# Running the first unit's half parts one weight piece at a time, with the recurrence between their steps

## The chip, the cores and the metric

The kernel runs on one core of one Trainium2 chip. The metric is the device time of one execution in microseconds (us), as the median of several. Before the change it was 684.3 us (4 runs, 682.91 to 685.18).

All arithmetic is fp32. The engines are TensorE (matrix products, PE in the profile, its weight loads PEld), VectorE (DVE), ScalarE (ACT), GpSimd (POOL), and the queue of transfers (SPq).

## The reference

A decaying recurrence (retention) is followed by a two-layer perceptron with leaky ReLU:

```python
gamma = 1.0 - 2.0 ** (-5.0 - np.arange(H))
for t in range(S):                                  # B=4, H=8, S=768, D=64
    state = gamma * state + einsum('bhd,bhe->bhde', k[:, :, t], v[:, :, t])
    y[:, :, t] = einsum('bhd,bhde->bhe', q[:, :, t], state) / sqrt(D)
x = y.transpose(0, 2, 1, 3).reshape(3072, 512)
h = x @ w_in                                        # (512, 2048)
out = np.maximum(0.01 * h, h) @ w_out               # (2048, 512)
```

The weights arrive as 64-bit floats, which the kernel turns into 32-bit ones itself.

## The kernel before

The sequence is cut into 6 chunks of 128 positions. For chunk c and batch b, TensorE computes **scores** (`ap`), VectorE masks them (`am`), and TensorE adds up three products in one PSUM tile (`yp`): **reads** of the old state (not in chunk 0), **values**, and the new **state**. VectorE then **takes** x and the state out of that tile. GpSimd scales v by decay rates beforehand.

```python
def stage_a(c, b):                       # scores, then the mask
    ps = two_banks(f"ap_{c}_{b}")
    for a in range(HP):
        for j in range(2):
            nc.tensor.matmul(ps[:, j, a, :], lhsT=x[ts(j, 64), 1, a, :], rhs=x[ts(j, 64), 0, a, :])
    nc.vector.tensor_tensor(out=am, in0=ps, in1=mask, op=ALU.mult)     # (views cut)

def stage_y(c, bs, xb):                  # reads, values, state for each b, then the taking
    ...
```

The perceptron works in units of 512 hidden columns. The products of a unit normally go by a scheme of seven block products that needs **sums** of weight blocks and **differences** of x blocks (VectorE work: `add_sums`, `differences`). At the very start those are not ready, so the first unit of chunks 0 and 1 goes directly, as four **half parts** (chunk 0 or 1, `th` = batches 0-1 or 2-3). Weights come in pieces of 512 KB; ScalarE (`next_powers`) and VectorE (`next_mantissas`) convert one piece each.

```python
def direct(c, u, x, g, th):
    for kh in range(2):
        for r in range(2):
            for i in range(2):
                for k in range(2):       # pieces 2*kh and 2*kh+1 alternate
                    nc.tensor.matmul(banks[r][:, i, :], lhsT=block(2*u, r + 2*kh)[:, k, ts(i, 128)],
                                     rhs=x[:, 2*kh + th, k, :], ...)
            if kh == 1: nc.scalar.activation(g[:, 2*r + th], banks[r], AF.Prelu, alpha=0.01)
            yield
```

The main program strings these together by hand, and the trace shows each engine's work in that order (TensorE's: scores at 4.63 us, products at 8.30, scores at 11.06, products at 14.23, half part at 16.64):

```python
for _ in range(3): next_powers()
scored(0, 0)(); read(0, 0)(); scored(0, 1)()
next_mantissas(); next_powers(); read(0, 1)(); next_mantissas()
run(direct(0, 0, xs[0][0], parts[0][1], 0),
    {1: [next_mantissas, next_mantissas, scored(0, 2)], 3: [scored(0, 3)]})
...
read(0, 2)(); read(0, 3)()
run(direct(0, 0, xs[0][0], parts[0][1], 1), {1: [scored(1, 0)], 3: [scored(1, 1)]})
...
read(1, 0, 1)(); next_mantissas(); next_mantissas()
run(direct(1, 0, xs[1][0], parts[1][1], 0), {1: [scored(1, 2)], 3: [scored(1, 3)]})
...
differences(*parts[0][1:]); read(1, 2, 3)(); next_mantissas()
run(direct(1, 0, xs[1][0], parts[1][1], 1), {0: [next_mantissas]})
```

## Time and profile before

| what | value |
|---|---|
| time, median | 684.3 us |
| span of the profiled execution | 682.1 us |
| TensorE busy | 661.7 us (97%) |
| TensorE idle after its first matmul, up to 100 us | 12.1 us |
| VectorE busy | 369.2 us (54%) |
| start of the second half part | 33.87 us |
| start of the first output stage (A_o) | 73.19 us |

The prediction shows the rows for TensorE's waits and for the slow array clock (0.91 and 0.67). Two more rows of TensorE's timeline matter later (start, length, engine, source line, operation, tiles, shapes, number, and in brackets the idle time before):

```profile
99.73 1.97 PE L315 MATMUL B_h<-t,w 128*128 128x256 f32 x8 [0.30 <-DVE w L283]
...
122.46 1.99 PE L315 MATMUL A_o<-g,w 128*128 128x256 f32 x8
```

Groups of this form start every 1.73 us when nothing waits. The first of these two starts 2.18 after the group ahead of it, 0.45 late, and the next one starts 1.81 after it: 0.53 lost for a bracket of 0.30. The second starts 0.20 late without any bracket, and the next one 1.83 after it. So the wait there cost more than its bracket shows. The weight loads stood still ahead of both groups (PEld idle for 0.67 and 0.44 us); that this is the reason was not tested.

### The profile page before, as it was taken

What the parts mean: (1) busy time and instruction counts of PE and PEld (TensorE: products, weight loads), DVE (VectorE), ACT (ScalarE), POOL (GpSimd) and SP (SyncE); (2) the same over time, 40 slices, a digit from 0 to 9 for tenths busy, and PEclk for the clock granted to TensorE, in tenths of its full rate; (3) what the DMA queues carried; (4) which work ended last, traced back from release to release, by engine and by line L of the source; (5) the groups of instructions that cost most, each with busy time, mean ns of one, the idle gap of its engine ahead of it and who ended that gap; (6) DMA issues with size and microseconds to landing.
All of it is one profiled execution on the core that took longest, in us unless ns stands there. A gap on an engine that the chain in (4) does not pass through costs nothing.

```text
span 682.1 us, 9555 instructions
## 1 busy us (share of the span) xinstructions
PE 661.7 (97%) x4112; PEld 577.8 (85%) x4112; DVE 369.2 (54%) x563; ACT 162.2 (24%) x271; POOL 27.2 (4%) x29
## 2 busy tenths in 40 slices
PE   5888999999999999999999999999999999999997
PEld 4677888888888888888888888888888888888886
DVE  3637898988888765703653533553451354341342
ACT  4122635545542001311210221220221130221210
POOL 1300000000001010100100100100000000000000
PEclk9899999999999999999999999999999999999999
DMA  8901222223412453100301300301300000100001
GB/s 344 380 2 63 93 93 93 89 66 124 153 34 92 124 184 123 67 0 13 111 1 63 124 1 0 125 0 62 124 1 0 1 1 16 46 1 0 1 1 62
DMA packets 15161, 49.11 MB, mean 72 GB/s; under 512 B 1680, under 2 KB 1680, under 8 KB 15120
## 3 DMA queue, kind: packets, MB, share of 16 engines
q1 hardware_dynamic: 15120, 48.51, 20.2%
q8 instruction: 32, 0.52, 0.3%
q14 instruction: 9, 0.07, 0.0%
HBM read 42.21 MB, written 6.29 MB: 71 GB/s over the span
## 4 chain that ended last, share of the span: by engine, by line
PE 95%; DVE 3%; DMA 1%; issue 0%; POOL 0%; SPq 0%; DVEq 0%; POOLq 0%
PE A_o L315 12%; PE B_o L315 12%; PE C_o L315 12%; PE B_h L315 11%; PE C_h L315 11%; PE A_h L315 11%; PE D_o L315 6%; PE D_h L315 6%; PE d L333 4%; PE ap L147 4%; PE yp L169 3%; PE yp L164 1%; PE yp L176 1%; DMA dec<-decay_dram 1%; DVE x L182 1%; DVE w L276 0%
## 5 line engine op out<-in xcount | busy, mean ns | idle before, releaser
L315 PE MATMUL A_h<-x,w 128*128 128x256 f32 x352 | 83.2, 379 | 0.0
L315 PEld LDWEIGHTS A_h<-x,w 128*128 128x128 f32 x352 | 66.9, 190 | 9.1
L315 PE MATMUL A_o<-g,w 128*128 128x256 f32 x288 | 68.1, 379 | 0.0
L315 PEld LDWEIGHTS A_o<-g,w 128*128 128x128 f32 x288 | 54.6, 190 | 7.9 <-ACT g L361 0.4
L346 ACT ACTIVATE g<-g 128x512 f32<-128x512 f32 x66 | 40.0, 629 | 75.9 <-DVE g L280 75.9
L280 DVE TENSOR_TENSOR m<-m,B_h 128x512 f32<-128x512 f32 x22 | 15.1, 685 | 56.9 <-PE B_h L315 56.9
L280 DVE TENSOR_TENSOR m<-m,B_o 128x512 f32<-128x512 f32 x16 | 10.9, 684 | 63.9 <-PE B_o L315 63.9
L182 DVE TENSOR_TENSOR x<-yp,dec 128x512 f32<-128x512 f32 x24 | 16.5, 688 | 53.1 <-PE yp L176 40.8
L351 ACT COPY m<-A_h 128x512 f32<-128x512 f32 x22 | 12.8, 583 | 135.6 <-PE A_h L315 97.8
L150 DVE TENSOR_TENSOR am<-ap,mask 128x1024 f32<-128x1024 f32 x24 | 28.6, 1220 | 27.4 <-PE ap L147 27.4
L315 PE MATMUL C_h<-t,w 128*128 128x256 f32 x176 | 42.2, 383 | 0.0
L315 PE MATMUL B_h<-x,w 128*128 128x256 f32 x176 | 42.2, 383 | 0.0
L315 PE MATMUL B_h<-t,w 128*128 128x256 f32 x176 | 41.7, 379 | 0.3 <-DVE w L283 0.3
L315 PE MATMUL D_h<-t,w 128*128 128x256 f32 x176 | 41.6, 379 | 0.0
L315 PE MATMUL C_h<-x,w 128*128 128x256 f32 x176 | 41.6, 379 | 0.0
L133 POOL TENSOR_TENSOR kv<-kv,dec 128x512 f32<-128x512 f32 x19 | 21.0, 1103 | 450.3 <-DMA kv<-in_kv_dram 273.3
L333 PE MATMUL d<-x,w 128*128 128x256 f32 x128 | 31.3, 400 | 7.4 <-DVE x L182 5.2
L315 PEld LDWEIGHTS B_h<-t,w 128*128 128x128 f32 x176 | 33.4, 190 | 5.2 <-issue 0.7
L315 PEld LDWEIGHTS C_h<-x,w 128*128 128x128 f32 x176 | 33.4, 190 | 4.5
L315 PEld LDWEIGHTS D_h<-t,w 128*128 128x128 f32 x176 | 33.4, 190 | 4.5
L315 PEld LDWEIGHTS C_h<-t,w 128*128 128x128 f32 x176 | 32.9, 190 | 5.0
L315 PEld LDWEIGHTS B_h<-x,w 128*128 128x128 f32 x176 | 32.9, 190 | 4.9 <-issue 0.3
(103 smaller groups left out, 1057.1 us busy)
## 6 DMA issues: line engine op xcount, KB each, us to landing
raw<-in_weights_dram SPq DMA_DIRECT2D x31, 512.0 KB, 3.4
qk<-in_qk_dram SPq DMA_DIRECT2D x19, 512.0 KB, 3.8
kv<-in_kv_dram SPq DMA_DIRECT2D x19, 512.0 KB, 4.8
out_dram<-o SPq DMA_DIRECT2D x24, 256.0 KB, 2.1
in<-in_qk_dram SPq DMA_DIRECT2D x3, 512.0 KB, 11.6
in<-in_kv_dram SPq DMA_DIRECT2D x3, 512.0 KB, 11.6
o_in<-in_qk_dram SPq DMA_DIRECT2D x2, 512.0 KB, 10.2
o_in<-in_kv_dram SPq DMA_DIRECT2D x2, 512.0 KB, 10.9
```

What stands on the lines that cost most here:

```text
L133: nc.gpsimd.tensor_tensor(out=v, in0=v, in1=gk.unsqueeze(2).to_broadcast([128, H, D]), op=ALU.mult)
L147: nc.tensor.matmul(ps[:, j, a, :], lhsT=x[ts(j, 64), 1, a, :], rhs=x[ts(j, 64), 0, a, :])
L150: nc.vector.tensor_tensor(out=am.rearrange("p j a t -> p (j a) t"), in0=ps.rearrange("p j a t -> p (j a) t"), in1=mask.unsqueeze(1).to_bro ...
L164: nc.tensor.matmul(ps[ts(i, 64), j, m, :], lhsT=st[b][ts(j, 64), a, :], rhs=x[ts(j, 64), 0, a, :], start=(m == 0), stop=False, skip_group_ ...
L169: nc.tensor.matmul(ps[ts(i, 64), j, m, :], lhsT=y[:, 1, 2 * a + j, :], rhs=am[:, j, a, :], start=(c == 0 and m == 0), stop=True, skip_grou ...
L176: nc.tensor.matmul(sp[ts(j, 64), a, :], lhsT=y[:, 0, 2 * a + j, :], rhs=y[:, 1, 2 * a + j, :], start=False, stop=True, skip_group_check=True)
L182: nc.vector.tensor_tensor(out=blocks, in0=ps[:, :, 0 : HP // 2, :], in1=gq, op=ALU.mult)
L280: nc.vector.tensor_tensor(out=out, in0=a, in1=b, op=ALU.add)
L315: nc.tensor.matmul(ps[:, i, :], lhsT=block(w, sa)[:, k, ts(i, 128)], rhs=rhs[:, k, :], start=(first and i == 0 and n == 0 and k == 0), sto ...
L333: nc.tensor.matmul(banks[r][:, i, :], lhsT=block(2 * u, r + 2 * kh)[:, k, ts(i, 128)], rhs=x[:, 2 * kh + th, k, :], start=(kh == 0 and i = ...
L346: nc.scalar.activation(g[:, i], g[:, i], AF.Prelu, alpha=0.01)
L351: nc.scalar.copy(out=got["m1"], in_=ps)
```

## The change

The intent is to let TensorE work while VectorE masks, takes and converts. It has four parts.

1. A half part goes in four steps, each with the four matmuls of one weight piece, which leave eight records in the trace (x8 in the row at 20.86 us below).
2. The pieces of the recurrence (`score`, `masked`, `reads`, `values`, `state`, `taken`) become functions of their own, and the program puts steps of a half part between them.
3. The sums of weights and the differences of x of this unit move from the output stages to places between the half parts.
4. The decay table goes in two transfers, 6 KB of rates ahead of the first kv and 256 KB later, and the order of later transfers shifts.

```diff
-        for kh in range(2):
-            for r in range(2):
-                for i in range(2):
-                    for k in range(2):
+        for step in range(4):
+            kh, k = divmod(step, 2)
+            for r in range(2):
+                for i in range(2):
...
+    load(0, 0, between=lambda: nc.sync.dma_start(out=dec[:, rates:], in_=decay[:, rates:]))
+    load(0, 1, between=lambda: nc.sync.dma_start(out=dec[:, :rates], in_=decay[:, :rates]))
...
     scored(0, 0)()
-    read(0, 0)()
+    products(0, [0])
     scored(0, 1)()
-    next_mantissas()
-    next_powers()
-    read(0, 1)()
+    next_powers()
+    taken(0, 0, x)
+    products(0, [1])
+    taken(0, 1, x)
+    next_powers()
     next_mantissas()
...
+    steps = direct(0, 0, x, parts[0][1], 1)
+    next(steps)
+    scored(1, 0)()
+    next(steps)
+    scored(1, 1)()
...
+    next(steps)
+    products(1, [0, 1])
+    next_mantissas()
+    run(steps, {})
...
+    taken(1, 0, x1)
+    taken(1, 1, x1)
+    last_difference(x)
```

More of the change, by code (lines that the diff above doesn't have):

```diff
@@ L115, with load @@
     AHEAD = 2
-    def load(c, b, place=None):
+    def load(c, b, place=None, between=lambda: None):
         if place is None:
@@ L126, in load @@
             y = flat[:, half : 2 * half].rearrange("p (s h d) -> p s h d", s=2, h=H)
+        heads[c, b] = x, y
         nc.sync.dma_start(out=x, in_=qk[c, b])
+        between()
         nc.sync.dma_start(out=y, in_=kv[c, b])
-        heads[c, b] = x, y
     def decay_v(c, b):
@@ L134, in decay_v, with score @@
                                 op=ALU.mult)
-    scores = {}
+    scores, sums_at = {}, {}
     def two_banks(name):
         return psum.tile([128, 2, HP, C], FP32, tag="att", bufs=2, name=name)
-    def stage_a(c, b):
+    def score(c, b):
         x = heads[c, b][0]
-        ps = two_banks(f"ap_{c}_{b}")
+        ps = scores[c, b] = two_banks(f"ap_{c}_{b}")
         for a in range(HP):
@@ L148, in stage_a, with masked @@
                                  rhs=x[ts(j, 64), 0, a, :])
-        am = scores[c, b] = work.tile([128, 2, HP, C], FP32, tag="am", bufs=2, name=f"am_{c}_{b}")
+    def masked(c, b):
+        am = work.tile([128, 2, HP, C], FP32, tag="am", bufs=2, name=f"am_{c}_{b}")
         nc.vector.tensor_tensor(
-            out=am.rearrange("p j a t -> p (j a) t"), in0=ps.rearrange("p j a t -> p (j a) t"),
+            out=am.rearrange("p j a t -> p (j a) t"),
+            in0=scores[c, b].rearrange("p j a t -> p (j a) t"),
@@ L152, in stage_a @@
             in1=mask.unsqueeze(1).to_broadcast([128, H, C]), op=ALU.mult)
-    def stage_y(c, bs, xb):
-        got = [(b, *heads.pop((c, b)), scores.pop((c, b)), two_banks(f"yp_{c}_{b}")) for b in bs]
-        more = c < NC - 1
-        pairs = [(j, m, i, 2 * m + i) for m in range(HP // 2) for j in range(2) for i in range(2)]
-        sums = {}
-        for b, x, _, _, ps in got:
-            for j, m, i, a in pairs if c > 0 else ():
-                nc.tensor.matmul(ps[ts(i, 64), j, m, :], lhsT=st[b][ts(j, 64), a, :],
-                                 rhs=x[ts(j, 64), 0, a, :], start=(m == 0), stop=False,
-                                 skip_group_check=True)
-        for _, _, y, am, ps in got:
-            for j, m, i, a in pairs:
-                nc.tensor.matmul(ps[ts(i, 64), j, m, :], lhsT=y[:, 1, 2 * a + j, :],
-                                 rhs=am[:, j, a, :], start=(c == 0 and m == 0), stop=True,
-                                 skip_group_check=True)
-        for b, _, y, _, ps in got:
-            sp = sums[b] = ps[:, 0, HP // 2 :, :].rearrange("p a (two d) -> p (a two) d", two=2)
-            for a in range(HP) if more else ():
-                for j in range(2):
-                    nc.tensor.matmul(sp[ts(j, 64), a, :], lhsT=y[:, 0, 2 * a + j, :],
-                                     rhs=y[:, 1, 2 * a + j, :], start=False, stop=True,
-                                     skip_group_check=True)
-        for b, _, _, _, ps in got:
-            th, o = divmod(b * C, N)
-            blocks = xb.rearrange("p (kh th) k n -> p kh th k n", th=2)[:, :, th, :, ds(o, C)]
-            nc.vector.tensor_tensor(out=blocks, in0=ps[:, :, 0 : HP // 2, :], in1=gq, op=ALU.mult)
-            sp = sums[b]
-            if more:
-                if c > 0:
-                    nc.vector.tensor_tensor(out=st[b], in0=st[b], in1=sp, op=ALU.add)
-                nc.vector.tensor_tensor(out=st[b], in0=st[b] if c > 0 else sp,
-                                        in1=gc.unsqueeze(2).to_broadcast([128, HP, D]),
-                                        op=ALU.mult)
@@ new lines, in masked, with reads @@
+        scores[c, b] = am
+    pairs = [(j, m, i, 2 * m + i) for m in range(HP // 2) for j in range(2) for i in range(2)]
+    def reads(c, b):
+        x = heads[c, b][0]
+        ps = sums_at[c, b] = two_banks(f"yp_{c}_{b}")
+        for j, m, i, a in pairs if c > 0 else ():
+            nc.tensor.matmul(ps[ts(i, 64), j, m, :], lhsT=st[b][ts(j, 64), a, :],
+                             rhs=x[ts(j, 64), 0, a, :], start=(m == 0), stop=False,
+                             skip_group_check=True)
@@ new lines, in values, with for_state, state @@
+    def values(c, b):
+        y, am, ps = heads[c, b][1], scores.pop((c, b)), sums_at[c, b]
+        for j, m, i, a in pairs:
+            nc.tensor.matmul(ps[ts(i, 64), j, m, :], lhsT=y[:, 1, 2 * a + j, :],
+                             rhs=am[:, j, a, :], start=(c == 0 and m == 0), stop=True,
+                             skip_group_check=True)
+    def for_state(ps):
+        return ps[:, 0, HP // 2 :, :].rearrange("p a (two d) -> p (a two) d", two=2)
+    def state(c, b):
+        y = heads.pop((c, b))[1]
+        sp = for_state(sums_at[c, b])
+        for a in range(HP) if c < NC - 1 else ():
+            for j in range(2):
+                nc.tensor.matmul(sp[ts(j, 64), a, :], lhsT=y[:, 0, 2 * a + j, :],
+                                 rhs=y[:, 1, 2 * a + j, :], start=False, stop=True,
+                                 skip_group_check=True)
@@ new lines, in taken @@
+    def taken(c, b, xb):
+        ps = sums_at.pop((c, b))
+        th, o = divmod(b * C, N)
+        blocks = xb.rearrange("p (kh th) k n -> p kh th k n", th=2)[:, :, th, :, ds(o, C)]
+        nc.vector.tensor_tensor(out=blocks, in0=ps[:, :, 0 : HP // 2, :], in1=gq, op=ALU.mult)
+        sp = for_state(ps)
+        if c < NC - 1:
+            if c > 0:
+                nc.vector.tensor_tensor(out=st[b], in0=st[b], in1=sp, op=ALU.add)
+            nc.vector.tensor_tensor(out=st[b], in0=st[b] if c > 0 else sp,
+                                    in1=gc.unsqueeze(2).to_broadcast([128, HP, D]), op=ALU.mult)
@@ L190, in stage_y, with products @@
+    def products(c, bs):
+        for f in (reads, values, state):
+            for b in bs:
+                f(c, b)
+    def stage_y(c, bs, xb):
+        products(c, bs)
+        for b in bs:
+            taken(c, b, xb)
             n = c * B + b + AHEAD
@@ L283, in minus, with add_sums, last_sum, differences @@
         nc.vector.tensor_tensor(out=out, in0=a, in1=b, op=ALU.subtract)
-    def add_sums(k):
+    def add_sums(k, last=True):
         a11, a21, a12, a22, s1, s2, s4 = (block(k, i) for i in range(7))
         plus(s1, a21, a22)
-        minus(a21, a11, a21)
         minus(s2, s1, a11)
         minus(s4, a12, s2)
-    def differences(x, t):
+        if last:
+            last_sum(k)
+    def last_sum(k):
+        minus(block(k, 1), block(k, 0), block(k, 1))
+    def differences(x, t, last=True):
         minus(t[:, 0], x[:, 1], x[:, 0])
@@ L296, in differences, with last_difference @@
         minus(t[:, 2], x[:, 2], t[:, 1])
+        if last:
+            last_difference(x)
+    def last_difference(x):
         minus(x[:, 1], x[:, 3], x[:, 1])
@@ L328, in direct @@
                  for r in range(2)]
-        for kh in range(2):
+        for step in range(4):
+            kh, k = divmod(step, 2)
             for r in range(2):
                 for i in range(2):
-                    for k in range(2):
-                        nc.tensor.matmul(
-                            banks[r][:, i, :], lhsT=block(2 * u, r + 2 * kh)[:, k, ts(i, 128)],
-                            rhs=x[:, 2 * kh + th, k, :], start=(kh == 0 and i == 0 and k == 0),
-                            stop=(kh == 1 and k == 1), skip_group_check=True)
-                if kh == 1:
+                    nc.tensor.matmul(
+                        banks[r][:, i, :], lhsT=block(2 * u, r + 2 * kh)[:, k, ts(i, 128)],
+                        rhs=x[:, 2 * kh + th, k, :], start=(step == 0 and i == 0),
+                        stop=(step == 3), skip_group_check=True)
+                if step == 3:
                     nc.scalar.activation(g[:, 2 * r + th], banks[r], AF.Prelu, alpha=0.01)
-                yield
+            yield
     def hidden(c, u, x, t, g, gd):
@@ L453, in do @@
             decay_v(c, b)
-            stage_a(c, b)
+            score(c, b)
+            masked(c, b)
         return do
@@ L470, in rounds @@
         return {i: [round_piece] for i in steps}
-    load(0, 0)
-    nc.sync.dma_start(out=dec, in_=decay)
-    load(0, 1)
-    for n in range(3):
-        load_piece(n)
+    rates = HP * C
+    load(0, 0, between=lambda: nc.sync.dma_start(out=dec[:, rates:], in_=decay[:, rates:]))
+    load(0, 1, between=lambda: nc.sync.dma_start(out=dec[:, :rates], in_=decay[:, :rates]))
+    load_piece(0)
+    load_piece(1)
+    load(0, 2, new_o("in2"))
+    load_piece(2)
     load_piece(3, tile_x("words").rearrange("p i k n -> p (i k n)")[:, 0 : 2 * W])
-    load(0, 2, new_o("in2"))
     load(0, 3, new_o("in3"))
@@ L481 @@
     load(1, 1, unit_tile(LATE[1], "in11"))
+    load(1, 2, unit_tile(LATE[0], "in12"))
     nc.vector.memset(mask, 1.0)
@@ L484 @@
                             base=0, pattern=[[1, 128]], channel_multiplier=-1)
-    for _ in range(3):
-        next_powers()
     xs = {0: new_x(0)}
@@ L492 @@
     parts = [new_g(0, 0)]
+    x, t = xs[0]
     scored(0, 0)()
-    read(0, 0)()
+    products(0, [0])
     scored(0, 1)()
+    next_powers()
[3 more added lines that the diff above has]
+    next_powers()
     next_mantissas()
     next_powers()
-    read(0, 1)()
-    next_mantissas()
-    run(direct(0, 0, xs[0][0], parts[0][1], 0),
-        {1: [next_mantissas, next_mantissas, scored(0, 2)], 3: [scored(0, 3)]})
-    load(1, 2, unit_tile(LATE[0], "in12"))
-    load(1, 3)
-    read(0, 2)()
-    read(0, 3)()
-    run(direct(0, 0, xs[0][0], parts[0][1], 1), {1: [scored(1, 0)], 3: [scored(1, 1)]})
-    next_powers()
+    load(1, 3)
+    scored(0, 2)()
+    steps = direct(0, 0, x, parts[0][1], 0)
+    next(steps)
+    reads(0, 2)
+    values(0, 2)
+    next_mantissas()
+    decay_v(0, 3)
+    score(0, 3)
+    state(0, 2)
+    next(steps)
+    next_mantissas()
+    masked(0, 3)
+    next_powers()
+    taken(0, 2, x)
+    next_mantissas()
+    next(steps)
+    reads(0, 3)
+    values(0, 3)
+    state(0, 3)
+    run(steps, {})
+    taken(0, 3, x)
+    add_sums(0, last=False)
+    differences(x, t, last=False)
+    steps = direct(0, 0, x, parts[0][1], 1)
+    next(steps)
+    scored(1, 0)()
+    next(steps)
+    scored(1, 1)()
+    next_powers()
+    next_mantissas()
+    next_powers()
+    next(steps)
+    products(1, [0, 1])
+    next_mantissas()
+    run(steps, {})
     next_powers()
@@ L510 @@
     parts.append(new_g(1, 0))
-    read(1, 0, 1)()
+    x1, t1 = xs[1]
+    taken(1, 0, x1)
+    taken(1, 1, x1)
+    last_difference(x)
+    scored(1, 2)()
+    steps = direct(1, 0, x1, parts[1][1], 0)
+    next(steps)
+    scored(1, 3)()
+    next(steps)
+    differences(*parts[0][1:])
+    next(steps)
+    products(1, [2, 3])
     next_mantissas()
+    next_powers()
+    run(steps, {})
+    taken(1, 2, x1)
+    taken(1, 3, x1)
     next_mantissas()
-    run(direct(1, 0, xs[1][0], parts[1][1], 0), {1: [scored(1, 2)], 3: [scored(1, 3)]})
     next_powers()
+    differences(x1, t1, last=False)
+    run(direct(1, 0, x1, parts[1][1], 1), {1: [next_mantissas]})
     next_powers()
-    differences(*parts[0][1:])
-    read(1, 2, 3)()
-    next_mantissas()
-    run(direct(1, 0, xs[1][0], parts[1][1], 1), {0: [next_mantissas]})
-    next_powers()
-    next_powers()
+    last_sum(0)
     differences(*parts[1][1:])
+    last_difference(x1)
     for u in range(NU):
@@ L535 @@
             at = rounds(1, 4) if u < NU - 1 else {}
-            if u == 0:
-                put(at, s2=[differ(c)])
-                if c == 0:
-                    put(at, s3=[lambda: add_sums(0)])
+            if u == 0 and c == 0:
+                at = rounds(4)
             if u == NU - 1 and NC > 2:
```

## The prediction

> **What bounds the kernel now.** I read the page first, then TensorE's timeline over the first 100 us, then VectorE's over the same stretch, then the view of busy time by stretch.
>
> ```profile
> PE 661.7 (97%) x4112; PEld 577.8 (85%) x4112; DVE 369.2 (54%) x563; ACT 162.2 (24%) x271; POOL 27.2 (4%) x29
> ...
> PE   5888999999999999999999999999999999999997
> ```
>
> TensorE is busy for 661.7 of 682.1 us, so all its idle time is 20.4 us, 3.0% of the span. The row by slices says where: the first four slices (17 us each) hold nearly all of it. The change touches the code up to about 100 us only, and leaves the number of matmuls alone. What it can win is idle time there, and clock.
>
> ```profile
> 14.23 1.09 PE L169 MATMUL yp<-am,kv 128*64 128x128 f32 x16 [1.38 <-issue]
> ...
> 19.48 4.85 PE L333 MATMUL d<-x,w 128*128 128x256 f32 x14 [2.14 <-DVE w L276]
> ...
> 33.87 3.72 PE L333 MATMUL d<-x,w 128*128 128x256 f32 x16 [0.78 <-DVE x L182]
> ...
> 44.76 0.67 PE L164 MATMUL yp<-in,st 64*64 64x128 f32 x16 [0.73 <-DVE am L150]
> ...
> 50.06 3.69 PE L333 MATMUL d<-x,w 128*128 128x256 f32 x16 [1.80 <-DVE x L182]
> ...
> 66.21 7.15 PE L333 MATMUL d<-x,w 128*128 128x256 f32 x32 [1.80 <-DVE x L182]
> ```
>
> The number in brackets is TensorE's idle time before the group, and what ended it. Of all brackets in this view: 4.63 for the first load, then 1.59, 1.38, 0.85, 2.14, 0.78, 0.73, 1.80, 0.73, 1.80 and, at 99.73, 0.30. After the first matmul that is 12.1 us. The two pairs of 0.73 and 1.80 have one form: scores (ap) are followed at once by the recurrence (yp), which waits for the mask on VectorE; and the recurrence is followed at once by a half part (d), which waits for VectorE to bring x out of PSUM. The 2.14 is another: weights not yet converted.
>
> ```profile
> 17.28 0.69 DVE L274 SCALAR_TENSOR_TENSOR w<-raw,w 128x512 f32<-128x512 uint32 x1
> 18.08 1.34 DVE L276 SCALAR_TENSOR_TENSOR w<-w,z 128x512 f32<-128x512 f32 x1
> 19.35 0.41 DVE L272 TENSOR_SCALAR w<-raw 128x512 uint32<-128x512 uint32 x1
> 19.80 0.69 DVE L274 SCALAR_TENSOR_TENSOR w<-raw,w 128x512 f32<-128x512 uint32 x1
> ```
>
> One piece of weights costs VectorE 0.41 + 0.69 + 0.69 and small gaps, some 1.95 us. One here took 1.34.
>
> ```profile
> 16.00:20.00 4.00, 1.22 (x3) 0.80 (x4) 3.83 (x7) 2.58 (x5) 1.44 (x1) 0.91 1.03 406
> 20.00:24.00 4.00, 4.00 (x14) 3.19 (x12) 3.63 (x5) 0.00 (x0) 1.20 (x2) 0.67 1.02 410
> ```
>
> Per stretch: width, then busy time of TensorE, its weight loads, VectorE, ScalarE, GpSimd, then clock. At 16 to 24 us VectorE has 3.83 and 3.63 us of work in 4 us: it is the bound there, not TensorE. The clock falls to 0.91 and 0.67 after the idle 2.14, and the 14 records of d take 4.85 us where 16 take 3.72 later (3.25 for 14): 1.6 us lost.
>
> [...] the first scores take 2.08 us, the later ones 1.16; the dip above costs 3.2 us at half speed. [...] the 1.34 at 18.08 and a 1.41 at 21.66 are the same operations that take 0.69 elsewhere, and GpSimd's value scaling (L133) ran at 17.44 to 18.88 and 21.38 to 22.53. [...] the trace has 680 to 690. So moving sums and differences costs VectorE nothing new, it only changes when.
>
> **The change part by part.** TensorE's pieces, warm, from its timeline: a half part d is 32 records, 7.3 us, now in four steps of 8 records, 1.83 each; scores ap 1.1; one batch's yp of chunk 0 1.55 (values 1.03, state 0.5); the two batches of chunk 1 together 4.16 (43.36 to 48.25 less 0.73). VectorE: mask 1.25, taking x and state of chunk 0 1.1, of chunk 1 1.45, one piece 1.95, one sum or difference 0.69.
>
> *Up to the first half part (now 16.64).* The decay rates that GpSimd needs come in a small transfer of their own before kv, so scaling starts when kv lands instead of at 7.20. But the mask ends at 8.05 anyway, so the first values move from 8.30 to about 8.15: 0.15 won. Then mask(0,1) comes before the taking of (0,0) on VectorE. The second products use the PSUM tile that the taking must free (two buffers, scores and sums in turn). So: scores end 12.75, mask 14.0, taking 15.1, values start at 15.15, not 14.23: 0.9 lost. Products end 16.85; scores of (0,2) fill 16.85 to 18.0.
>
> *The first half part.* VectorE's chain, in program order: taking (0,1) 16.9 to 18.0, piece 0 to 19.95, mask (0,2) to 21.2, piece 1 to 23.2, plus about 0.65 where GpSimd's scaling of a landing kv falls on it, piece 2 to 25.8 (26.4 with a second collision), mask (0,3) to 27.6, taking (0,2) to 28.7, piece 3 to 30.7. TensorE: step 0 at 19.95 (to 21.8), values (0,2), scores (0,3), state (0,2) to 24.5, step 1 to 26.35, step 2 to 28.25, values and state (0,3) from 28.8 to 30.4, step 3 from 30.7 to 32.5. If a cold spell as now falls on it, TensorE is up to 1.6 us later in the middle, of which the waits behind absorb a third or so. I put the start of the second half part at 32.8, against 33.87 now: 1.1 won. TensorE's work is spread between VectorE's, but VectorE's chain from 16.9 to 30.7 is nearly unbroken: it becomes the bound, and so the gain here is small.
>
> *The three other half parts (33.87 to 73.19 now, 39.3).* Work: three times 7.3, four scores 4.4, two double products 8.3: 34.6. The idle in it is 0.73 + 1.80 + 0.73 + 1.80 = 5.06, which accounts for the rest within 0.4. In the new order a step of d (1.83) stands between the scores and the recurrence, against a mask of 1.25: both 0.73 vanish. Between the products and the next half part stand step 3 (1.85) and, after the first pair, scores (1.1): together 2.95 against the 2.15 that VectorE needs until the second x. That 1.80 vanishes too. After the second pair only step 3 stands there, 1.85 against 2.15: 0.3 stays. So 4.8 won by the sum of idle, 4.4 by the difference of span and work; I take 4.4.
>
> *VectorE in that stretch.* Over 28 us after 32.8 it has masks, takings and pieces much as now, plus the six operations of add_sums and differences moved forward (4.1 us). I count 22 to 24 us of work: it fits, with little slack near the end. At the first output stage (A_o, now at 73.19, then about 67.7) VectorE has some 7 us of queue left: part of piece 8, last_sum, four differences, and the last difference of x. The first thing that the stage needs from it, u2, then comes at about 75; TensorE needs that bank again five products later, at 67.7 + 5 x 1.73 = 76.4. It holds by 1.4 us.
>
> *The output stages.* Twelve operations on x and weights (8.2 us) leave them for earlier places, so the wait of 0.30 at 99.73 goes.
>
> Sum: 0.15 - 0.9 is inside the 1.1; 1.1 + 4.4 + 0.3 = 5.8 us of 684.05, so 678.3. After 100 us TensorE has no gap of note (578.4 busy of 582), and nothing there changes.
>
> **Rivals.** (a) *VectorE takes over as the bound from 17 to 76 us.* For it: it is full already at 16 to 24 us, and the new order puts more into 17 to 70. Against: between 33.87 and 48.30 it is busy only 3.19 of 14.43 us, so there is room for all that moves. If it does, the first part wins nothing and u2 comes late: 2 to 3 us won in all, 681.5. (b) *Every gap is closed.* The order of mask and taking at 13 us does no harm, and the clock stays warm because TensorE's work is spread: then the first part wins 3 us or more, 8 in all, 676. Against: piece 0 cannot be ready before VectorE has taken (0,1). (c) *The transfers.* Pieces 4 and later wait for a buffer that piece 0's conversion frees, now some 4 us later, and stand in one queue with the last inputs. Against: before, ScalarE first touches piece 4 at 42.87, VectorE at 50.61, and nothing is in flight from 36 us on; a landing near 30 is early enough for a use near 40. If it went wrong, VectorE would stall at piece 4 and the time would be as now.
>
> **Range and chances.** The certain part is 4 to 5 us (the waits of one form); the first part is worth between -1 and +3. That gives 676.3 to 681.0. Runs of before spread over 682.91 to 685.18, which the range leaves room for. Two per cent is 13.7 us; all the idle after the first matmul is 12.1 and the cold spells add 3 to 4, so faster by 2% would need all of it: 0.01. For slower nothing new is computed: 0.01.
>
> **What would show it.** In the changed trace: A_o starts at 67 to 68.5 instead of 73.19; no waits of TensorE on the mask near 40 to 60 us; one wait of at most 0.5 before the last half part of chunk 1; between 16.9 and 31 us VectorE idle under 2 us, and TensorE's waits there named after weights (L276 now) or the taking; values (0,1) at about 15.1, waiting for the taking. I am wrong if the second half part starts at 34 or later, or at 31 or before; if TensorE waits on u2 or on sums in the output stages; or if a gap appears after 100 us.

Where the text is marked as cut, here and in the expectation of e6, it spoke of the hardware without a trace or run of this case to show it. No term of the sum went with the cuts: it came to 1.1 + 4.4 + 0.3 = 5.8 us. The dip is a granted clock of 0.50 from 19.25 to 22.66 us, 3.2 us of it from the start of the 14 records at 19.48; the trace shows the slow operations of VectorE only as overlapping GpSimd's in time, not why; and 680 to 690 are the ns of one VectorE sum or difference of two 128x512 fp32 tiles (L283).

## The result, and the profile after

| kernel | median us | executions | ratio to before |
|---|---|---|---|
| before | 684.3 | 682.91 to 685.18 (4) | 1 |
| changed | 676.72 | 676.07, 676.70, 676.73, 678.18 | 0.9894 (0.9871 to 0.9917) |

A ratio here is the mean time of one kernel's fast runs over that of the other's of the same rounds, so not quite the ratio of the medians quoted. The measured 676.72 lies inside the predicted 676.3 to 681.0 and 1.6 us below the predicted value. The profiled execution is the slowest of the four (678.18); that turns out to matter.

The page of the changed kernel, the busy time of the engines and the chain that ended last by engine:

```profile
PE 662.4 (98%) x4112; PEld 580.1 (86%) x4112; DVE 371.4 (55%) x563; ACT 162.6 (24%) x271; POOL 27.2 (4%) x29
...
PE 97%; DMA 1%; DVE 0%; issue 0%; POOL 0%; SPq 0%; DVEq 0%; POOLq 0%
```

The same chain in the kernel before, in which VectorE still had 3%:

```profile
PE 95%; DVE 3%; DMA 1%; issue 0%; POOL 0%; SPq 0%; DVEq 0%; POOLq 0%
```

As many TensorE records as before take nearly the same time (662.4 us, 661.7 before), in a span of 676.2 instead of 682.1. TensorE's timeline in the first 100 us:

```profile
8.85 1.97 PE L174 MATMUL yp<-am,kv 128*64 128x128 f32 x16 [2.53 <-POOL kv L134]
...
15.06 1.98 PE L174 MATMUL yp<-am,kv 128*64 128x128 f32 x16 [1.37 <-issue]
...
20.86 3.40 PE L366 MATMUL d<-x,w 128*128 128x256 f32 x8 [1.87 <-DVE w L299]
...
32.29 3.72 PE L366 MATMUL d<-x,w 128*128 128x256 f32 x16
...
59.38 9.02 PE L366 MATMUL d<-x,w 128*128 128x256 f32 x40
68.24 1.89 PE L347 MATMUL A_o<-g,w 128*128 128x256 f32 x8
```

Three brackets remain after the first matmul: 2.53, 1.37 and 1.87. From 20.86 us on there is none up to the output stages: the two pairs of 0.73 and 1.80, the 0.78 and the 0.30 are gone. The row at 32.29 holds step 3 of the first half part and step 0 of the second. The second half part therefore starts at about 34.2, not earlier than before (33.87), while A_o starts at 68.24 instead of 73.19. In this execution everything was won behind 34 us, and nothing in front of it.

The front shows why. Busy time by stretch of four microseconds (TensorE, its weight loads, VectorE, ScalarE, GpSimd, granted clock, share of transfers, GB/s):

```profile
16.00:20.00 4.00, 2.99 (x42) 2.68 (x38) 2.04 (x4) 2.49 (x5) 1.04 (x1) 1.00 1.03 408
20.00:24.00 4.00, 3.14 (x8) 2.21 (x8) 3.76 (x6) 1.26 (x2) 1.04 (x1) 0.66 1.03 410
```

At 20 to 24 us the clock is 0.66, and step 0, eight records, takes 3.40 us; the same eight take 1.99 in the rows at full clock. At 16 to 20 us VectorE has only 2.04 us of work, and then TensorE waits for it:

```profile
13.73 1.23 DVE L153 TENSOR_TENSOR am<-ap,mask 128x1024 f32<-128x1024 f32 x1 [6.07 <-PE ap L148]
14.87 0.68 DVE L195 TENSOR_TENSOR x<-yp,dec 128x512 f32<-128x512 f32 x1
15.47 0.41 DVE L200 TENSOR_TENSOR st<-yp,dec 128x256 f32<-128x256 f32 x1
17.92 0.69 DVE L195 TENSOR_TENSOR x<-yp,dec 128x512 f32<-128x512 f32 x1 [2.04 <-PE yp L186]
18.53 0.41 DVE L200 TENSOR_TENSOR st<-yp,dec 128x256 f32<-128x256 f32 x1
18.86 0.42 DVE L295 TENSOR_SCALAR w<-raw 128x512 uint32<-128x512 uint32 x1
```

VectorE idles for 2.04 us before taking x of (0,1) and begins piece 0 only after it, at 18.86, although ScalarE had finished its part of piece 0 at 14.13. In the kernel before, piece 0 was converted in that gap (14.05 to 15.98).

### The profile page after: what moved, and what is told of

Same layout as the page of the kernel before. It is cut to its first block, busy times and chain, and to the rows that moved or that the text cites. A ratio compares the mean times of both kernels' runs of the same rounds, so it can differ in the third digit from the quotient of the medians.

```text
span 676.2 us, 9567 instructions
## 1 busy us (share of the span) xinstructions
PE 662.4 (98%) x4112; PEld 580.1 (86%) x4112; DVE 371.4 (55%) x563; ACT 162.6 (24%) x271; POOL 27.2 (4%) x29
## 4 chain that ended last, share of the span: by engine, by line
PE 97%; DMA 1%; DVE 0%; issue 0%; POOL 0%; SPq 0%; DVEq 0%; POOLq 0%
PE B_o L347 12%; PE A_o L347 12%; PE C_o L347 12%; PE B_h L347 11%; PE C_h L347 11%; PE A_h L347 11%; PE D_o L347 6%; PE D_h L347 6%; PE d L366 5%; PE yp L174 4%; PE ap L148 3%; PE yp L167 2%; PE yp L186 2%; DMA kv<-in_kv_dram 1%; POOL kv L134 0%
## 5 line engine op out<-in xcount | busy, mean ns | idle before, releaser
L303 DVE TENSOR_TENSOR m<-m,B_h 128x512 f32<-128x512 f32 x22 | 15.1, 686 | 57.1 <-PE B_h L347 57.1
L153 DVE TENSOR_TENSOR am<-ap,mask 128x1024 f32<-128x1024 f32 x24 | 28.6, 1220 | 17.8 <-PE ap L148 17.8
L306 DVE TENSOR_TENSOR gd<-g,gd 128x512 f32<-128x512 f32 x48 | 34.8, 725 | 1.8
```

The costliest lines, as they stand in the source:

```text
L153: nc.vector.tensor_tensor(out=am.rearrange("p j a t -> p (j a) t"), in0=scores[c, b].rearrange("p j a t -> p (j a) t"), in1=mask.unsqueeze ...
L303: nc.vector.tensor_tensor(out=out, in0=a, in1=b, op=ALU.add)
L306: nc.vector.tensor_tensor(out=out, in0=a, in1=b, op=ALU.subtract)
```

## The experiments

The theory after the result: the order of the three later half parts carries 5 us or more of the gain. The front is worth little, because what the interleaving wins there is taken back by the late piece 0, by a later first kv, and by the slow clock. Rivals: the steps by pieces carry the gain; the moved sums and differences carry it; or the clock alone does. Twelve kernels were run, all in five rounds, all correct. The medians of the kernel before were 684.66, 684.57 and 684.75.

| label | what it is | median us | lowest to highest | ratio (95% interval) |
|---|---|---|---|---|
| e1_front_only | new front, old later part | 682.46 | 682.44 to 682.93 | 0.9970 (0.9958 to 0.9983) |
| e6_steps_only | before, with steps by pieces | 682.21 | 680.67 to 683.51 | 0.9961 (0.9947 to 0.9976) |
| e2_front_old | old front with steps, new later part | 675.33 | 674.49 to 676.93 | 0.9864 (0.9846 to 0.9881) |
| e3_sums_back | changed, sums as before | 677.25 | 676.63 to 677.39 | 0.9890 (0.9876 to 0.9903) |
| e9_scores_adjacent | changed, no step ahead of the recurrence | 679.05 | 677.51 to 679.33 | 0.9913 (0.9899 to 0.9927) |
| e10_steps_before | changed, no step behind it | 679.00 | 678.84 to 680.58 | 0.9925 (0.9912 to 0.9939) |
| e4_dec_first | changed, decay table first | 676.53 | 674.57 to 676.80 | 0.9875 (0.9861 to 0.9889) |
| e5_dec_as_before | changed, decay table as before | 676.51 | 675.94 to 677.36 | 0.9882 (0.9868 to 0.9896) |
| e7_warm | changed, with filler matmuls | 674.73 | 673.63 to 675.11 | 0.9852 (0.9839 to 0.9865) |
| e11_old_front_warm | e2 with filler matmuls | 673.72 | 672.82 to 674.79 | 0.9841 (0.9826 to 0.9856) |
| e13_piece0_early | changed, piece 0 early | 674.41 | 673.69 to 675.71 | 0.9847 (0.9834 to 0.9861) |
| e14_early_dec_warm | changed, with e13, e5 and filler | 672.16 | 672.03 to 672.44 | 0.9818 (0.9805 to 0.9831) |

Since kernels of different calls ran on different chips, differences between them are best taken between their ratios: 0.001 is 0.68 us. The changed kernel has the widest interval (four executions), so a difference from it is uncertain by 1.8 to 2.0 us (an estimate from the two intervals). Small differences from it rest on the waits in the traces more than on the times.

### Which part carries the gain: e1, e2, e6

**e1_front_only** keeps the new front (transfers, steps, interleaved first half part) and restores the rest.

```diff
-    steps = direct(0, 0, x, parts[0][1], 1)
-    next(steps)
-    scored(1, 0)()
...
+    run(direct(0, 0, xs[0][0], parts[0][1], 1), {1: [scored(1, 0)], 3: [scored(1, 1)]})
+    ... (as in the kernel before, up to the first output stage; sums and differences in the output stages)
```

> The changed front (transfers, pieces in steps, up to the end of the first half part) with the old order of the three later half parts and the old places of sums and differences. Theory: the gain of about 7.5 us comes almost wholly from the waits of 0.73 and 1.80 in the three later half parts, and the front is worth 0 to 1.5: this kernel at 682.5 to 684.5 us, and the profile shows the two pairs of 0.73 and 1.80 again. Rival: the steps by pieces carry 3 us or more of it: below 681.

It measured 682.46, at the lower end of the theory's range (0.04 below it). The new front alone is worth 0.0030, or 2.1 us, more than the 0 to 1.5 that the theory gave it. The two pairs of 0.73 and 1.80 are back in its trace, to the hundredth.

**e2_front_old** is the reverse: the transfers and the order of the old front up to the second half part, then the new order. The four steps of a half part stay.

```diff
-    products(0, [0])
+    read(0, 0)()
     scored(0, 1)()
...
+    next_mantissas()
+    next_powers()
+    read(0, 1)()
+    next_mantissas()
+    run(direct(0, 0, xs[0][0], parts[0][1], 0),
+        {1: [next_mantissas, next_mantissas, scored(0, 2)], 3: [scored(0, 3)]})
```

> The old front with the new order from the second half part on, sums and differences in their new places. Theory: 5.0 from the later half parts and 0.3 from the output stage: 678.5 to 679.5 us. Rival (the front carries the gain): 681 or more.

It measured 675.33, faster than expected by 3 us: neither the theory nor the rival holds. On the same chip it is 1.9 us faster than e3_sums_back, which has the new front. So the old front, given the steps, is probably the better one, by about 2 us; the intervals of the two overlap slightly.

**e6_steps_only** asks what in that front did it: the kernel before with nothing but the new order of the sixteen matmuls in `direct`.

> The kernel before, with one thing changed: the sixteen matmuls of a half part go in four steps, one piece of weights each. Theory (clock): with one piece ready TensorE then has 8 records of work at 17 us instead of 2, its wait for the second piece falls from 2.14 to about 1.0, and the array keeps its full clock, which together is worth the 1.9 us by which the second half part began earlier in the run with the old front and the new later order: 682.0 to 683.0 us, and its records of d at 17 to 24 us take 0.23 us each in most executions. Rival: [...] the step order is worth only the 1.1 of waiting at most: 683.5 to 684.5.

It measured 682.21, as the theory said. TensorE's timeline of e6 at the place where the kernel before had a wait of 2.14 and then 4.85 us for 14 records:

```profile
16.63 1.99 PE L333 MATMUL d<-x,w 128*128 128x256 f32 x8 [0.85 <-DVE x L182]
19.67 1.99 PE L333 MATMUL d<-x,w 128*128 128x256 f32 x8 [1.05 <-DVE w L276]
```

Eight records instead of two fit in front of the wait, the wait halves, and the granted clock of this execution was 1.00 in every stretch up to 36 us. The steps alone are worth 0.0039, 2.7 us; the whole new front was worth 0.0030. The two intervals overlap, but with the new later part behind them the order is the same (e2 against the changed kernel, 0.0030 apart): nothing shows that the rest of the new front earned anything, and the best estimates are that it cost 0.6 to 2 us.

### The waits behind 34 us: e9, e10, e3

**e9_scores_adjacent** takes away the step between scores and recurrence, twice.

```diff
     next(steps)
+    next(steps)
     scored(1, 1)()
...
-    next(steps)
     products(1, [0, 1])
```

> The changed kernel, with the second scores of each pair of chunk 1 moved from before step 2 to after it, so that no step stands between scores and recurrence. Theory: the two waits of 0.73 for the mask come back: 1.2 to 1.6 us above the changed kernel's 676.7, so 678.0 to 678.3. Rival: something else hides the mask: 676.5 to 677.

It measured 679.05, 0.0019 or 1.3 us above the changed kernel by the ratios: inside the 1.2 to 1.6 expected, while the median lies above the 678.3 expected. TensorE's timeline shows three waits after 34 us:

```profile
41.15 0.67 PE L167 MATMUL yp<-in,st 64*64 64x128 f32 x16 [0.73 <-DVE am L153]
...
55.46 0.67 PE L167 MATMUL yp<-qk,st 64*64 64x128 f32 x16 [0.73 <-DVE am L153]
...
62.12 7.14 PE L366 MATMUL d<-x,w 128*128 128x256 f32 x32 [1.24 <-ACT w L283]
```

The two waits for the mask are exactly those of the kernel before, 1.46 of the 2.70 in all. The third was not expected: the mask now comes later on VectorE, four differences and piece 6 queue behind it (to 60.0), and the taking of x behind those; the second x is out at 61.97. The bracket names ScalarE, whose part of this half part's four pieces had long been done: the first half part uses the same four, and its step 3 is in a row that starts at 30.27. The neighbouring rows have to be read to see which wait it was.

**e10_steps_before** moves step 3 of two half parts ahead of the products.

```diff
-    next(steps)
-    products(1, [0, 1])
-    next_mantissas()
     run(steps, {})
+    products(1, [0, 1])
+    next_mantissas()
     ... (the same in the next half part)
```

> The changed kernel, with step 3 of the second and third half parts moved ahead of the recurrence's products, so that only scores (first pair) or nothing (second pair) stand between the products and the next half part. Theory: waits for x of about 0.9 to 1.1 and 1.8 to 2.2 come back: 2.7 to 3.3 above 676.7, so 679.4 to 680.0. Rival: under 678.5.

It measured 679.00, 0.0031 or 2.1 us above the changed kernel, and so between the theory's 679.4 and the rival's 678.5. The two waits in its trace:

```profile
46.70 1.16 PE L148 MATMUL ap<-in 64*128 64x128 f32 x16 [0.70 <-PE yp L186]
...
61.93 7.14 PE L366 MATMUL d<-x,w 128*128 128x256 f32 x32 [1.81 <-DVE x L195]
```

Together they are 2.5, against 2.7 to 3.3 expected. The first is a wait of scores and not of d: the bracket names TensorE, but the scores start 0.1 after VectorE's last reading of the first batch's PSUM tile (L199, done at 46.60), and the second x is out only at 47.66. The second wait is of the size expected; the first was put too large.

**e3_sums_back** keeps the new order, with all sums and differences in the output stages again.

```diff
-    add_sums(0, last=False)
-    differences(x, t, last=False)
...
-            if u == 0 and c == 0:
-                at = rounds(4)
+            if u == 0:
+                put(at, s2=[differ(c)])
+                if c == 0:
+                    put(at, s3=[lambda: add_sums(0)])
```

> The changed kernel with all sums and differences (and piece 8) in the output stages as before. Theory: they are worth only the wait of 0.30 at the end of the output stages: 0 to 0.5 us above the changed kernel's 676.7, so 676.5 to 677.5. Rival: moving them off the output stages gave 1 us or more: 678 or above.

It measured 677.25, with a ratio 0.0004 from the changed kernel's, in the other direction: no difference that can be told. The wait that I had put down to the sums (0.30 at 99.73) does not come back with them. In e3 the conversion of piece 11 stands a little earlier in relation to A_o (21.1 us behind it, 22.5 before). In the new order the sums could have stayed where they were. In the old order they were not tested alone; there four differences stand in the chain just ahead of piece 11 (93.01 to 95.74).

### The start and the clock: e4, e5, e7

**e4_dec_first** sends the whole decay table in one transfer ahead of the first kv.

```diff
-    load(0, 0, between=lambda: nc.sync.dma_start(out=dec[:, rates:], in_=decay[:, rates:]))
-    load(0, 1, between=lambda: nc.sync.dma_start(out=dec[:, :rates], in_=decay[:, :rates]))
+    load(0, 0, between=lambda: nc.sync.dma_start(out=dec, in_=decay))
+    load(0, 1)
```

> The changed kernel, with the decay table as one transfer ahead of the first kv instead of 6 KB ahead of kv and 256 KB later. Theory: the 6 KB transfer of 48 bytes a row costs more queue time than its bytes (kv landed at 7.61 against 5.84 before), so one transfer of 262 KB lets kv land by 6.7, the first values start at 7.8 instead of 8.85, and the time falls by 0.5 to 1.0: 675.7 to 676.2. Rival: what delays kv is the order and the rate at the start, not the small rows: kv lands at 7.3 or later and the time stays at 676.7 plus or minus 0.3.

The median is 676.53, and three of four executions lie at 676.44 to 676.80. The first values started at 8.54, and kv landed 5.6 us after an issue at 1.70, at 7.3: that is what the rival said, and the 6 KB of small rows are not to blame. GpSimd needs the last of the first three transfers in every order. In the fourteen profiles, read from GpSimd's start, the table (262 KB) lands at 6.6 to 7.4 us where it is the third; kv (512 KB) lands at 7.3 to 7.8 where it is the third, be it behind 6 KB or 262 KB. So what is shown is the place in the queue, and the third place is earlier for the table.

The fourth execution, the profiled one, took 674.57 at a clock of 1.000. Its step 0:

```profile
18.38 1.99 PE L366 MATMUL d<-x,w 128*128 128x256 f32 x8 [1.88 <-DVE w L299]
```

The same wait of 1.88 precedes it as in the changed kernel, and yet the eight records take 1.99, not 3.40. So one order of work, in one kernel, meets the slow clock or not from execution to execution (the mean clock is 1.000 in this one and 0.997 in the other three), and here these executions are 2 us apart.

**e5_dec_as_before** restores the old transfers of the table: `load(0, 0)`, the table, `load(0, 1)`.

> The changed kernel with the decay table as one transfer after the first kv, as in the kernel before. Theory: the 6 KB transfer delays kv by more than it brings the rates forward: the first values start at 8.1 to 8.5 (8.85, 8.69 and 8.49 in the runs with the split), and the time falls by 0.2 to 0.5 against 676.7. Rival: the start of the values there does not reach the end, because VectorE and piece 0 bound what follows: 676.5 to 677.

The first values started at 8.35, as expected. The median of 676.51 is 0.0012 in ratio below the changed kernel, 0.8 us, but the intervals overlap widely; half of its executions lie above 677. It is inconclusive: at most a few tenths are shown.

**e7_warm** puts filler matmuls on a constant tile into TensorE's waits. Their result is not read.

```diff
+    fill(10)
     scored(0, 0)()
+    fill(8)
     products(0, [0])
     scored(0, 1)()
+    fill(5)
...
     scored(0, 2)()
+    fill(8)
     steps = direct(0, 0, x, parts[0][1], 0)
```

> The changed kernel with 31 filler matmuls on a constant tile in TensorE's waits before 21 us (10 ahead of the first scores, 8, 5 and 8 after it); their result is not read. Theory: the slow clock in the front costs the changed kernel 2 us in most executions (its own fast executions and those of relatives lie 2 us apart, with a clock of 1.000 and 0.997), and further time in the first 13 us: the filler makes the clock full from 8 us on, time 672.5 to 674.5 and the spread of executions under 0.5. Rival: VectorE and the transfers bound the front and the clock does not matter: 676 to 677.

It measured 674.73, 0.2 above the theory's range and well below the rival's: 0.0042 or 2.9 us below the changed kernel, though the work on TensorE grew. The values of (0,1) in its timeline:

```profile
12.79 1.09 PE L174 MATMUL yp<-am,kv 128*64 128x128 f32 x16
```

They start at 12.79 instead of 15.06, and take 1.09 instead of 1.98. (The seven other profiles of this front or a variant of it, without filler, have 13.85 to 15.25; the changed kernel's is one of the slowest.) TensorE's speed in the front is a cause of its own. (The expectation, like that of e11, puts the slow first 13 us down to the clock. That was inference: the granted clock reads 1.00 there with and without filler, and what is shown is the durations.) The spread, however, did not fall under 0.5: the executions lie at 673.63 to 675.11.

### Piece 0, and a better version: e13, e11, e14

**e13_piece0_early** moves one call in the changed kernel.

```diff
     products(0, [1])
-    taken(0, 1, x)
     next_powers()
     next_mantissas()
+    taken(0, 1, x)
     next_powers()
```

> The changed kernel with one line moved: piece 0 is converted before the taking of (0,1), as in the kernel before, in the 2.0 us in which VectorE waits for the second products. Theory: the changed front is bound by VectorE from 18 us on, and piece 0 in its path is what cancels the gain from the interleaving; step 0 then starts right after x of (0,1), at 17.5 to 18.9 by the clock's state, instead of 20.86, and the wait of 1.9 ahead of it falls under 0.5: 674.8 to 675.8, and fewer slow executions. Rival: later VectorE work (collisions with GpSimd, piece 3) takes the time back: 676.3 to 676.9.

It measured 674.41, 0.0047 or 3.2 us below the changed kernel, a little more than expected, and no execution lies above 675.71. The wait ahead of step 0 did not fall under 0.5 in the profiled execution:

```profile
19.31 1.99 PE L366 MATMUL d<-x,w 128*128 128x256 f32 x8 [1.41 <-DVE x L195]
```

In that run the conversion met GpSimd's scaling of (0,2), at 16.20 to 17.30 (one operation at 16.44 took 1.41 instead of 0.69), and x of (0,1) was taken behind it. Still, step 0 came 1.5 us earlier than in the changed kernel's profile, and its eight records took 1.99 instead of 3.40. With this one line the changed front is no worse than the old one.

What the line does is not separated from the clock. All executions of e13 have a mean clock of 0.999 or 1.000, all of the changed kernel 0.997. And in the one execution of e4 at 1.000, with piece 0 still late (and another order of transfers), the time was 674.57, as fast as e13. Of the 3.2 us the trace shows 0.5 as less waiting (1.41 against 1.87) and 1.4 as the speed of step 0. Late piece 0 costs time together with the clock; how much it costs at full clock is open.

**e11_old_front_warm** is e2 with filler.

> The old front with steps by pieces and the new later order (675.33 before) plus 21 filler matmuls in the front. Theory: the first 13 us lose up to 2 us to the slow clock there too, so 672.5 to 674.0. Rival: conversion of the pieces on VectorE bounds this front from 14 us on whatever the clock: 674.5 to 675.5, with less spread.

It measured 673.72: inside the theory's range, 0.0023 or 1.6 us below e2.

**e14_early_dec_warm** combines the changed kernel with piece 0 early, the old transfers of the table, and filler (8, 8, 5 and 2 matmuls).

> The three together on the changed kernel: piece 0 early, one decay transfer after the first kv, 23 filler matmuls. Theory: gains add up in part, 671.5 to 673.5, faster than the changed kernel and than each alone. Rival: all three work on the same wait, so no better than the filler alone (674.7) by more than 0.5.

It measured 672.16, with all executions at 672.03 to 672.44, the narrowest spread, and a ratio of 0.9818 to the kernel before. It beats the changed kernel by 4.6 us in the medians and 0.0076, 5.2 us, in the ratios, and the filler alone (e7) by 0.0034, 2.3 us, so the rival is out. Its timeline:

```profile
12.84 1.09 PE L174 MATMUL yp<-am,kv 128*64 128x128 f32 x16
...
16.18 1.99 PE L366 MATMUL d<-x,w 128*128 128x256 f32 x8
...
26.62 3.72 PE L366 MATMUL d<-x,w 128*128 128x256 f32 x16
```

The last row holds step 3 of the first half part and step 0 of the second, so the second half part starts at about 28.5, against 34.2 in the changed kernel's profile. What is left before it is the first transfer (4.8 us, in which only filler runs), scores that still take 2.08 us behind it instead of 1.16, and one wait of 0.57 for the inputs of (0,3).

## Why the prediction was right or wrong

The time was inside the range and 1.6 us below the predicted value. Between the two profiled executions the gain is 5.9 us (682.1 less 676.2), almost the 5.8 predicted, and that is luck: the front gave 1.4 less than predicted there, and the parts behind it 1.3 more. The steps, one by one:

**What bounds the kernel** held. The gain is idle time before 100 us and clock.

**Up to the first half part: two steps failed.** "Scaling starts when kv lands instead of at 7.20" was right in words, but kv landed at 7.61, so the scaling started at 7.75 and the first values at 8.85: 0.55 lost where 0.15 was to be won. (Over all profiles without filler the first values start at 8.08 to 8.64 with the old order of transfers and at 8.49 to 9.04 with kv third.) I had left out that the small transfer pushes kv to third place in the queue. And "the second products use the PSUM tile that the taking must free" was wrong. Values of (0,1) started at 15.06, while VectorE was still taking x of (0,0) (14.87 to 15.55): they waited for the mask alone (13.73 to 14.96). What fits this, and was not tested, is that they got the buffer of the scores, which the mask had freed first. The predicted 15.15 was met by another way: 0.55 from kv and 0.3 from slow scores. The 0.9 was never lost; a start at the right time is not evidence for its cause.

**The first half part** was put at 1.1 us of gain, starting the second at 32.8. The profiled execution has 34.2, which I had named as a sign of being wrong. It is the slowest of the four: in it the products up to 17.8 us took nearly twice as long as later (the values of (0,1) 1.98 us instead of 1.09), and the granted clock was 0.50 from 21.29 to 24.70. In e3, which has the same front and a span of 674.7 (two of the changed kernel's other executions have 674.8), it starts at 32.3. The front is worth 2.1 us by e1. "VectorE's chain becomes the bound" fits e13, where one move of piece 0 in that chain won 3.2 us, though part of that went by way of the clock. What I failed to ask is whether the chain had to be in that order: the 2.0 us in which VectorE waits for the second products were in my own timetable, between 15.1 and 16.9.

**The three later half parts** were mis-sized: 4.4 us predicted, 5.3 measured (39.5 us from 33.87 to A_o before, 34.2 us from 34.2 to A_o after, by the chain that ended last). Of the two sums in the prediction the one by idle time was right (5.06). The 0.3 that was to stay did not: VectorE begins to take the first batch's x at 59.03, before the second batch's products end, and has the second x by 61.1, when step 3 ends. e9 and e10 show both kinds of wait coming back when a step is taken away.

**The output stages** were put at 0.3, for the sums that leave them. The measured gain is about 0.75: A_o to B_h took 26.4 us before and 25.9 after, and B_h to the next A_o 22.7 and 22.45. The wait for weights at 99.73 cost more than its bracket shows (0.53 for 0.30). The cause does not hold in the new order: e3 has the sums back and does not have the wait of 0.30.

**u2** was begun at 74.30, done at 74.98, and its bank was needed at 76.87. The step held, by 1.9 us instead of the 1.4 predicted.

**The rivals.** "VectorE takes over" was true of the front only. "The clock stays warm because TensorE's work is spread" was half right: with the steps the old front keeps the clock (0.999 or 1.000 in all six executions of e6, 0.995 to 0.998 in the eleven of the kernel before beside them), and the changed front, with piece 0 late and no filler, loses it again in most executions (0.996 or 0.997 in 27 of 31). The length of a wait alone does not explain it: the slow records came behind waits of 2.14 us in the kernel before and 1.87 to 2.01 in kernels with the changed front, and e4 had the same wait of 1.88 without them. "The transfers" did not matter for pieces 4 and later, as argued.

The sum was then 0.9 short in the later half parts, 0.4 in the output stages, and 1.0 in the front. That gives 8.1 us against the measured 7.6 (medians) or 7.3 (ratio); the terms come from different executions and agree no better than that. Nor do they add up quite: behind the old front with steps (e6 to e2) the later part is worth 0.0097, 6.6 us, behind the new one (e1 to the changed kernel) 0.0076, 5.2 us, with intervals of about 1 us on each.

What stays open: why the third transfer lands so late at the start, and what decides in which executions the clock falls. That filler makes the kernel faster is shown, and in e4 the execution without the fall was the fastest. But the mean clock does not explain the spread of executions: a run of the kernel before at 1.000 was the slowest of its nine (685.41), one of e10 at 1.000 the slowest of its five (680.58), and the four of e2, all at 1.000, lie 2.4 us apart.

## What to carry to other kernels

Put independent TensorE work between a product and the VectorE pass that it waits for, and size it against that pass: here a step of 1.83 us hid a mask of 1.22 us, and 5 us of 684 went with two such rearrangements. When VectorE becomes the bound of a stretch, list its own waits too; one line that fills a wait of 2 us with work that is needed next (3.2 us, the clock's share included) was worth about as much as the whole new front (2.1 us), or more. At the start of a kernel, where TensorE waits in short bursts, order its work so that the bursts are long (2.7 us in e6, its shorter wait included), or fill the waits: 1.6 us (e11) and 2.9 us (e7) here, with unread matmuls.

## What the traces showed of the start

- In the changed kernel TensorE started at 4.24 us and its products ran at about half speed up to 17.8 us (from the values of (0,1) to the next products 1.73 us, 15.06 to 16.79, against 0.90 in e7, 12.79 to 13.69), with a stretch of unbroken work from 8.85 to 13.68 in between. With filler from 1.12 us on, full speed came after 4.0 us of unbroken work in e7 (scores at 5.11 take 1.16) and 5.7 us in e14 (filler at 6.84, 16 records in 2.05).
- The granted clock in these profiles does not show the slow start: in the kernel before it reads 1.00 at 4 to 8 us, where scores take 2.08 us instead of 1.16. The durations have to be compared. It does show the later dip (0.50 from 19.25 to 22.66 us).
- Unread filler matmuls took 2.9 us off the time here, 0.4% (e7).
- 6 KB ahead of the first kv moved its landing from 5.84 to 7.61 us, and 262 KB in the same place moved it to 7.3 (one profile each).
